# Attention and a maxout feed-forward: four visits to the scores in a group with four score banks, in place of three visits with six

## The chip, the cores and the metric

The kernel runs on one core of a Trainium2 chip. The core has TensorE for matmuls (PE in the profile; PEld is its loading of weights), VectorE (DVE), ScalarE (ACT), GpSimd (POOL) and SyncE (SP); here POOL and SP only issue transfers, apart from a few constants at the start. Matmuls write to PSUM, which has eight banks of 2 KB in each of 128 partitions; VectorE and ScalarE read them from there. The metric is the time of one execution on the device, in microseconds, the median over runs.

## What is computed

An attention whose softmax has one more term in the denominator, and then a feed-forward that takes the largest of three products:

```python
# q, k, v: (8 batches, 12 heads, 448 positions, 64)
scores = matmul(q, k.T) / sqrt(64)
m = max(scores);  e = exp(scores - m)
attn = e / (sum(e) + exp(-m) + 1e-9)
x = matmul(attn, v)                      # -> 3584 tokens x 768
h = maximum(maximum(x @ w1, x @ w2), x @ w3)      # 768 x 768 each
out = h @ w_out                          # 3584 x 768, float32
```

Without the maximum this is `exp(s) / (sum(exp(s)) + 1)`, and that is how the kernel computes it. It works in float16 with float32 sums.

## The kernel before

**Tiling.** The 12 heads of a batch are three groups of four; 8 batches make 24 groups, numbered `i` from 0 to 23. A batch has 448 positions, four chunks of 112 keys. Within a group, heads go in two pairs (`pr`), because two heads of 64 rows fill the 128 rows of TensorE.

**A group's steps.** `copy_qk` and `pair_qk` (L133 to L149) copy a pair's k and q on VectorE into the order that a transpose wants. The transpose runs on TensorE for groups below `PE_TR = 7` (`pe_transpose_pair`, L151, with a copy from PSUM to `qkT` at L162), later as a DMA on the SP queue (`dma_transpose_pair`, L165). `scores_visit` (L174) computes score units: a unit is a pair and a key chunk, two matmuls of 448 columns (L187) into a tile `stp` of two PSUM banks; then ScalarE takes the exponential of each tile into `eT` (L196). `av_group` (L205) makes three products of 16 matmuls each (L216), four at a time in 32 columns of TensorE: the denominator with a matrix of ones, and the even and the odd half of the numerator. VectorE copies each out of PSUM (`den` L226, `num` L231), ScalarE makes 1/(den + 1) as exp(-ln) (`lnd` L235, `rb` L237), and `normalize` (L239) multiplies into `xT`, two multiplications (L240).

**The feed-forward in pieces.** A batch's feed-forward is a list `pieces`: 18 up pieces (`up_piece`, six matmuls at L325 each, then a copy or a maximum into `hT` on VectorE, L333 and L335) and then output pieces (`out_piece`, six matmuls at L366, a scaling at L373, and stores on the SP queue at L389), six for an even batch and eight for an odd one. `moe(cols)` (L413) adds `cols` to a credit and issues pieces while the credit is above zero. After each piece it takes one job from the list `jobs`; jobs are VectorE's `normalize` steps and the copies and DMA transposes for the group after next, so that they do not stand in a row ahead of the pieces' evictions.

**PSUM.** `ps1` has two tiles of one bank (transposes, AV products, pieces), `ps2` two tiles of two banks and `ps3` one tile of two banks (both for `stp`; in batch 0 `ps3` holds the denominator). That is eight banks.

**Order.** The program is written in the order in which each engine is to run it; no scheduler moves it. Batch 0 is attended in two halves of the queries (`scores_half`, `av_half`), its order is a string of letters, `start` (L452), and its feed-forward is made of `up_half` pieces (L344). From group 3 on, a loop (L467) runs three visits in a group, with score units 0 to 2, 3 to 5, and 6 and 7:

```python
scores_visit(i, (0, 1, 2))
normalize = av_group(i - 1)          # from group 4 on; pieces in group 3
scores_visit(i, (3, 4, 5))
moe(gap)
next_pair(0)                         # moe(gap), with the transposes of the next groups
scores_visit(i, (6, 7))
moe(gap)
next_pair(1)
```

`add_pieces(b - 1)` runs in a batch's first group after `next_pair(0)`, and `gap` is then what the list holds, divided by 12 (a group has four calls of `moe(gap)`). After the loop follow the last AV, what is left in the list, and the last batch's feed-forward. The loads of q, k and v for group `i + 3` are issued at the head of group `i`, from POOL's queue.

Of the kernel before, what the change touches and what calls it, by code (L numbers as in the profile page):

```python
# [10 lines left out]
FP32 = mybir.dt.float32  # L11
FP16 = mybir.dt.float16
AF = mybir.ActivationFunctionType
ALU = mybir.AluOpType
ts = bass.ts

MMDT = FP16
# [4 lines left out]
def kernel(  # L22
# [11 lines left out]
    nc = tc.nc  # L34
# [30 lines left out]
    ht_pool = ctx.enter_context(tc.tile_pool(name="ht", bufs=2))  # L65
    out_pool = ctx.enter_context(tc.tile_pool(name="outp", bufs=3))

    ps1 = ctx.enter_context(tc.tile_pool(name="ps1", bufs=2, space=bass.MemoryType.PSUM))
    ps2 = ctx.enter_context(tc.tile_pool(name="ps2", bufs=2, space=bass.MemoryType.PSUM))
    ps3 = ctx.enter_context(tc.tile_pool(name="ps3", bufs=1, space=bass.MemoryType.PSUM))  # L70

    ctx.enter_context(tc.manual_schedule())

# [56 lines left out]

    state = {}

    def copy_qk(i, pr, n):  # L133
        st = state.setdefault(i, {"qk16": {}, "qkT": {}})
        if n == 0:
            st["qk16"][pr] = p16_pool.tile(
                [SC, 2, NCH, 2, D], MMDT, tag="qk16", name="qk16"
            )
        if i == 0 and pr == 0:
            src = first["kq"[n]]  # L140
        else:
            src = raw[i]["kq"[n]][:, 2 * pr : 2 * pr + 2]
        nc.vector.tensor_copy(
            out=st["qk16"][pr][:, n], in_=src.rearrange("p h c d -> p c h d")
        )

    def pair_qk(i, pr):
        for n in range(2):
            copy_qk(i, pr, n)  # L149

    def pe_transpose_pair(i, pr):  # L151
        st = state[i]
        qk16 = st["qk16"].pop(pr)
        trT = ps1.tile([128, 2, S], MMDT, tag="bank1", name="trT")
        for n in range(2):
            for c in range(NCH):
                nc.tensor.transpose(  # L157
                    out=trT[:, n, ts(c, SC)], in_=qk16[:, n, c, :, :],
                    identity=ident16[0:SC, 0:SC],
                )  # L160
        qkT = att_pool.tile([2 * D, 2 * S], MMDT, tag="qkT", name="qkT")
        nc.vector.tensor_copy(out=qkT, in_=trT.rearrange("p n s -> p (n s)"))  # L162
        st["qkT"][pr] = qkT

    def dma_transpose_pair(i, pr):  # L165
        st = state[i]
        qkT = att_pool.tile([2 * D, 2 * S], MMDT, tag="qkT", name="qkT")
        nc.sync.dma_start_transpose(
            out=qkT.rearrange("p (n s) -> p n s", s=SC),
            in_=st["qk16"].pop(pr).rearrange("p n c h d -> p (n c h d)"),  # L170
        )
        st["qkT"][pr] = qkT

    def scores_visit(i, units):  # L174
        st = state[i]
        if "eT" not in st:
            st["eT"] = e_pool.tile([SC, GH, NCH, S], MMDT, tag="eT", name="eT")
        stps = []
        for u in units:
            pr, c = divmod(u, NCH)  # L180
            qkT = st["qkT"][pr]
            if u in (2, 5):
                stp = ps3.tile([128, 2, 512], FP32, tag="bank3", name="stp")
            else:
                stp = ps2.tile([128, 2, 512], FP32, tag="bank2", name="stp")
            for hh in range(2):
                nc.tensor.matmul(  # L187
                    out=stp[:, hh, 0:S],
                    lhsT=qkT[hh * D : hh * D + D, c * SC : c * SC + 128],
                    rhs=qkT[hh * D : hh * D + D, S : 2 * S],  # L190
                    start=True,
                    stop=True,
                )
            stps.append((pr, c, stp))
        for pr, c, stp in stps:
            nc.scalar.activation(  # L196
                out=st["eT"][:, 2 * pr : 2 * pr + 2, c, :],
                in_=stp[0:SC, :, 0:S],
                func=AF.Exp,
                scale=scale,  # L200
            )
# [3 lines left out]
    def av_group(i):  # L205
        b, g = groups[i]
        st = state.pop(i)
        eT, v16 = st["eT"], raw[i].pop("v")
        if g == 0:
            xT[b] = xt_pool.tile([128, NDC, S], MMDT, tag="xT", name="xT")  # L210

        def col_tiled(weights):
            bank = ps1.tile([128, 512], FP32, tag="bank1", name="av")
            for c in range(NCH):
                for hh in range(GH):
                    nc.tensor.matmul(  # L216
                        out=bank[32 * hh : 32 * hh + 32, 0:S],
                        lhsT=weights(hh, c),
                        rhs=eT[:, hh, c, :],
                        start=(c == 0),  # L220
                        stop=(c == NCH - 1),
                    )
            return bank

        den = small.tile([128, S], FP32, tag="den", name="den")
        nc.vector.tensor_copy(  # L226
            out=den, in_=col_tiled(lambda hh, c: ones16[:, :])[:, 0:S]
        )
        num = small.tile([128, 2, S], FP32, tag="num", name="num")
        for hf in range(2):  # L230
            nc.vector.tensor_copy(  # L231
                out=num[:, hf], in_=col_tiled(lambda hh, c: v16[:, hh, c, hf::2])[:, 0:S]
            )
        lnd = small.tile([128, S], FP32, tag="lnd", name="lnd")
        nc.scalar.activation(out=lnd, in_=den, func=AF.Ln, bias=one_b)  # L235
        rb = small.tile([128, S], FP32, tag="rb", name="rb")
        nc.scalar.activation(out=rb, in_=lnd, func=AF.Exp, bias=ln_lam, scale=-1.0)  # L237

        def normalize(hf):  # L239
            nc.vector.tensor_tensor(  # L240
                out=xT[b][:, 2 * g + hf, :], in0=num[:, hf], in1=rb, op=ALU.mult
            )

        return normalize


    def scores_half(i, pr, half):
# [28 lines left out]
    def av_half(i, half):  # L276
# [6 lines left out]
        def col_tiled(out, weights):  # L283
# [7 lines left out]
                        stop=(c == NCH - 1),  # L291
                    )

        den = ps3.tile([128, 2, 512], FP32, tag="bank3", name="den")[:, 0]
        num = ps1.tile([128, 512], FP32, tag="bank1", name="num")
        col_tiled(den[:, 0:HQ], lambda hh, c: ones16[:, :])
        lnd = small.tile([128, S], FP32, tag="lnd", name="lnd")
        nc.scalar.activation(  # L298
# [3 lines left out]
        nc.scalar.activation(  # L302
            out=rb[:, 0:HQ], in_=lnd[:, 0:HQ], func=AF.Exp, bias=ln_lam, scale=-1.0
        )
        for hf in range(2):
            col_tiled(num[:, ts(hf, HQ)], lambda hh, c: v16[:, hh, c, hf::2])
        for hf in range(2):
# [91 lines left out]
    def add_pieces(b):  # L399
        for fc in range(NFC):  # L400
            for i in range(3):
                pieces.append((up_piece, (b, fc, i), NDC * (S + 6)))
        add_out(b)

    credit = [0.0]
    jobs = []

    def flush():
        while jobs:
            f, a = jobs.pop(0)  # L410
            f(*a)

    def moe(cols):  # L413
        credit[0] += cols
        while pieces and credit[0] > 0:
            f, a, w = pieces.pop(0)
            f(*a)
            credit[0] -= w
            if jobs:
                f, a = jobs.pop(0)  # L420
                f(*a)
        if not pieces:
            credit[0] = min(credit[0], 0.0)


    NI = len(groups)
    PE_TR = 7
    UP_H = 2 * NDC * (HQ + 6)
# [38 lines left out]
    for i in range(NG, NI):  # L467
        b, g = groups[i]
        if i == 3:
            load_group(5, "qk")  # L470
            load_group(4, "v")
            load_weight(3)
            load_group(5, "v")
            load_group(6)
        elif i + 3 < NI:
            load_group(i + 3)
        on_pe = i + 1 < PE_TR
        if i == NG:
            gap = sum(w for f, a, w in pieces) / 15

        def next_pair(pr):
            if i + 2 >= PE_TR and i + 2 < NI:
                for n in range(2):
                    jobs.append((copy_qk, (i + 2, pr, n)))
                jobs.append((dma_transpose_pair, (i + 2, pr)))
            if on_pe:
                pair_qk(i + 1, pr)
            moe(gap)
            if on_pe:
                pe_transpose_pair(i + 1, pr)  # L490

        scores_visit(i, (0, 1, 2))
        normalize = None
        if i > NG:
            normalize = av_group(i - 1)
        else:
            moe(gap)
        scores_visit(i, (3, 4, 5))
        if i > NG:
            for hf in range(2):  # L500
                jobs.append((normalize, (hf,)))
        moe(gap)
        next_pair(0)
        if i > NG and g == 0:
            flush()
            add_pieces(b - 1)
            gap = sum(w for f, a, w in pieces) / 12
        scores_visit(i, (6, 7))
        moe(gap)
        next_pair(1)  # L510
        flush()
    normalize = av_group(NI - 1)
    for hf in range(2):
        jobs.append((normalize, (hf,)))
    moe(float("inf"))
    flush()
    add_pieces(B - 1)
    moe(float("inf"))

# [29 lines left out]
```

## Time and profile before

| | before |
|---|---|
| median of 3 runs | 360.43 us (360.41 to 360.69) |
| the profiled execution's own time | 360.69 us |
| its span, first to last instruction | 358.9 us |
| granted TensorE clock | 0.999 |
| TensorE busy | 341.4 us, 3148 matmuls |
| VectorE busy | 213.4 us, 430 instructions |
| ScalarE busy | 192.7 us, 247 instructions |
| GpSimd busy | 58.1 us |
| DMA moved | 40.75 MB |

The profile is of one execution. Its page gives each engine's busy time, the span in 40 slices, and the chain of waits that ended last. In rows of instructions, a line such as "L325 PE MATMUL p_i<-xT" names the line of the kernel, the engine, the operation, the tile written and those read. A row of the timeline has the start, the duration, and in brackets how long the engine stood idle before it and what released it. In the chain in order of time, a row is the start, how long the chain lay there, and what ran: for TensorE one stretch of matmuls of the same line. Matmuls overlap each other in the array, so the duration of one (353 ns) is longer than the distance between two (189 ns).

### The profile page before, as it was taken

What the parts mean: (1) busy time and instruction counts of PE and PEld (TensorE: products, weight loads), DVE (VectorE), ACT (ScalarE), POOL (GpSimd) and SP (SyncE); (2) the same over time, 40 slices, a digit from 0 to 9 for tenths busy, and PEclk for the clock granted to TensorE, in tenths of its full rate; (3) what the DMA queues carried; (4) which work ended last, traced back from release to release, by engine and by line L of the source; (5) the groups of instructions that cost most, each with busy time, mean ns of one, the idle gap of its engine ahead of it and who ended that gap; (6) DMA issues with size and microseconds to landing.
All of it is one profiled execution on the core that took longest, in us unless ns stands there. A gap on an engine that the chain in (4) does not pass through costs nothing.

```text
span 358.9 us, 7470 instructions
## 1 busy us (share of the span) xinstructions
PE 341.4 (95%) x3148; PEld 178.2 (50%) x3148; DVE 213.4 (59%) x430; ACT 192.7 (54%) x247; POOL 58.1 (16%) x90
## 2 busy tenths in 40 slices
PE   3879899999999999999999999999999999999994
PEld 2557777544444444444444544444445444445552
DVE  3334566676666666665657657656656655656553
ACT  3697567875563664663762863763764664630000
POOL 8424532220220220220220220220000000000000
PEclk9999999999999999999999999999999999999999
DMA  9999999489746964857739876759421540012006
GB/s 137 193 208 206 202 199 161 59 171 162 102 66 124 179 125 75 118 107 161 103 57 122 150 166 101 102 99 188 53 54 26 136 118 2 0 46 88 2 4 173
DMA packets 71617, 40.75 MB, mean 114 GB/s; under 512 B 33824, under 2 KB 66848, under 8 KB 71584
## 3 DMA queue, kind: packets, MB, share of 16 engines
q0 software_dynamic: 35072, 21.01, 42.9%
q1 hardware_dynamic: 36272, 19.05, 22.2%
q8 instruction: 24, 0.39, 0.4%
q10 hardware_dynamic: 240, 0.23, 0.2%
q14 instruction: 9, 0.07, 0.1%
HBM read 42.47 MB, written 11.01 MB: 149 GB/s over the span
## 4 chain that ended last, share of the span: by engine, by line
PE 91%; ACT 2%; DVE 2%; DMA 2%; issue 1%; POOL 1%; DVEq 0%; POOLq 0%
PE p_i L325 41%; PE op_ps L366 15%; PE av L216 15%; PE stp L187 11%; PE p_i L344 6%; DMA ld_k<-in_k_dram 2%; PE trT L157 2%; ACT eTh L269 1%; PE stp L260 1%; PE num L286 1%; PE den L286 1%; ACT rb L302 0%; DVE xT L308 0%; ACT lnd L298 0%; DVE qkT L162 0%
## 5 line engine op out<-in xcount | busy, mean ns | idle before, releaser
L196 ACT ACTIVATE eT<-stp 112x896 f16<-112x896 f32 x168 | 141.9, 912 | 109.3 <-PE stp L187 109.3
L335 DVE TENSOR_TENSOR hT<-hT,p_i 128x448 f16<-128x448 f16 x84 | 52.2, 622 | 43.5 <-PE p_i L325 43.5
L366 PE MATMUL op_ps<-w_130,hT 128*128 128x384 f16 x336 | 57.9, 327 | 0.0
L325 PE MATMUL p_i<-xT,w_127 128*128 128x448 f16 x252 | 54.7, 353 | 0.0
L325 PE MATMUL p_i<-xT,w_129 128*128 128x448 f16 x252 | 54.6, 353 | 0.0
L325 PE MATMUL p_i<-xT,w_128 128*128 128x448 f16 x252 | 54.6, 353 | 0.0
L89 POOL DMA_DIRECT2D ld_v<-in_v_dram x24 | 17.0, 709 | 177.0 <-PE stp L187 171.8
L366 PEld LDWEIGHTS <-hT 128*128 128x128 f16 x336 | 31.6, 98 | 25.1 <-issue 3.0
L187 PE MATMUL stp<-qkT 64*128 64x448 f16 x336 | 42.7, 353 | 0.0
L373 DVE TENSOR_SCALAR o_sb<-op_ps 128x384 f32<-128x384 f32 x56 | 31.1, 556 | 18.4 <-PE op_ps L366 18.4
L216 PE MATMUL av<-eT,ld_v 112*32 112x448 f16 x672 | 38.8, 353 | 0.0
L333 DVE CAST hT<-p_i 128x448 f16<-128x448 f32 x42 | 26.2, 625 | 20.8 <-PE p_i L325 20.8
L325 PEld LDWEIGHTS <-w_127 128*128 128x128 f16 x252 | 23.6, 98 | 25.2 <-issue 4.4
L325 PEld LDWEIGHTS <-w_129 128*128 128x128 f16 x252 | 23.9, 98 | 24.7 <-issue 3.3
L325 PEld LDWEIGHTS <-w_128 128*128 128x128 f16 x252 | 23.9, 98 | 24.7 <-issue 3.3
L231 DVE COPY num<-av 128x448 f32<-128x448 f32 x42 | 26.2, 625 | 8.8 <-PE av L216 6.0
L269 ACT ACTIVATE eTh<-stp 112x896 f16<-112x896 f32 x24 | 20.5, 912 | 12.7 <-PE stp L260 12.6
L216 PEld LDWEIGHTS <-ld_v 112*32 112x32 f16 x672 | 18.6, 97 | 16.5 <-issue 5.0
L240 DVE TENSOR_TENSOR xT<-num,rb 128x448 f16<-128x448 f32 x42 | 25.9, 617 | 0.0
L187 PEld LDWEIGHTS <-qkT 64*128 64x128 f16 x336 | 11.3, 94 | 24.6 <-issue 19.1
L226 DVE COPY den<-av 128x448 f32<-128x448 f32 x21 | 13.1, 625 | 16.1 <-PE av L216 16.1
L216 PE MATMUL av<-eT,ones_121 112*32 112x448 f16 x336 | 19.8, 355 | 0.0
(161 smaller groups left out, 225.6 us busy)
## 6 DMA issues: line engine op xcount, KB each, us to landing
ld_v<-in_v_dram POOLq DMA_DIRECT2D x24, 224.0 KB, 4.1
ld_q<-in_q_dram POOLq DMA_DIRECT2D x23, 224.0 KB, 5.1
ld_k<-in_k_dram POOLq DMA_DIRECT2D x23, 224.0 KB, 6.1
out_dram<-o_sb SPq DMA_DIRECT2D x8, 336.0 KB, 3.0
out_dram<-o_sb SPq DMA_DIRECT2D x8, 288.0 KB, 3.8
out_dram<-o_sb SPq DMA_DIRECT2D x8, 240.0 KB, 3.4
out_dram<-o_sb SPq DMA_DIRECT2D x8, 192.0 KB, 2.7
w_127<-in_moe_w_dram POOLq DMA_DIRECT2D x3, 384.0 KB, 11.9
```

What stands on the lines that cost most here:

```text
L187: nc.tensor.matmul(out=stp[:, hh, 0:S], lhsT=qkT[hh * D : hh * D + D, c * SC : c * SC + 128], rhs=qkT[hh * D : hh * D + D, S : 2 * S], sta ...
L196: nc.scalar.activation(out=st["eT"][:, 2 * pr : 2 * pr + 2, c, :], in_=stp[0:SC, :, 0:S], func=AF.Exp, scale=scale,)
L216: nc.tensor.matmul(out=bank[32 * hh : 32 * hh + 32, 0:S], lhsT=weights(hh, c), rhs=eT[:, hh, c, :], start=(c == 0), stop=(c == NCH - 1),)
L231: nc.vector.tensor_copy(out=num[:, hf], in_=col_tiled(lambda hh, c: v16[:, hh, c, hf::2])[:, 0:S])
L240: nc.vector.tensor_tensor(out=xT[b][:, 2 * g + hf, :], in0=num[:, hf], in1=rb, op=ALU.mult)
L269: nc.scalar.activation(out=st[key][:, 2 * pr : 2 * pr + 2, 2 * n : 2 * n + 2, :], in_=stp[0:SC, :, 0:S].rearrange("p h (c q) -> p h c q", ...
L325: nc.tensor.matmul(out=p_i[:, 0:S], lhsT=w_sb[i][:, dc, ts(fc, 128)], rhs=xT[b][:, dc, :], start=(dc == 0), stop=(dc == NDC - 1),)
L333: nc.vector.tensor_copy(out=dst, in_=p_i[:, 0:S])
L335: nc.vector.tensor_tensor(out=dst, in0=dst, in1=p_i[:, 0:S], op=ALU.max)
L344: nc.tensor.matmul(out=p_i[:, ts(j, HQ)], lhsT=w_sb[i][:, dc, ts(2 * fp + j, 128)], rhs=xT[b][:, dc, ts(half, HQ)], start=(dc == 0), stop= ...
L366: nc.tensor.matmul(out=op_ps[:, 0:NW], lhsT=hT[bp][:, fc, ts(t, 128)], rhs=wout_sb[:, fc, ts(nh, NW)], start=(fc == 0), stop=(fc == NFC - 1),)
L373: nc.vector.tensor_scalar(out=o_sb[:, ts(nh, NW)], in0=op_ps[:, 0:NW], scalar1=1.0 / LAMBDA, scalar2=None, op0=ALU.mult,)
```

## The change

The loop from group 3 on gets four visits with two score units each: a pair and half of its key chunks (`visits`). The score tiles have four banks (`ps2` alone); `ps3` is gone, and `ps1` has four tiles. AV's three products are not copied out of PSUM: ScalarE reads the denominator there, and VectorE multiplies the numerators from there, at once and without the list of jobs, which is gone. The copies for a DMA transpose stand directly ahead of it. `add_pieces` comes right after the AV that ends a batch, ahead of the second visit. The amount of pieces in a visit follows from a fixed rate, `steady` (in group 3 from what is left of batch 0): the credit for the first visit is reduced by the columns of an AV, and where a transpose runs on TensorE its columns are taken off. `start` and the order of batch 0 stay as they are; its denominators go to `ps1` instead of `ps3`.

```diff
-    ps1 = ctx.enter_context(tc.tile_pool(name="ps1", bufs=2, space=bass.MemoryType.PSUM))
+    ps1 = ctx.enter_context(tc.tile_pool(name="ps1", bufs=4, space=bass.MemoryType.PSUM))
     ps2 = ctx.enter_context(tc.tile_pool(name="ps2", bufs=2, space=bass.MemoryType.PSUM))
-    ps3 = ctx.enter_context(tc.tile_pool(name="ps3", bufs=1, space=bass.MemoryType.PSUM))
...
     def dma_transpose_pair(i, pr):
+        pair_qk(i, pr)
...
-    def scores_visit(i, units):
+    def scores_visit(i, pr, cs):
...
-        for u in units:
-            pr, c = divmod(u, NCH)
-            qkT = st["qkT"][pr]
-            if u in (2, 5):
-                stp = ps3.tile([128, 2, 512], FP32, tag="bank3", name="stp")
-            else:
-                stp = ps2.tile([128, 2, 512], FP32, tag="bank2", name="stp")
+        for c in cs:
+            stp = ps2.tile([128, 2, 512], FP32, tag="bank2", name="stp")
...
-        den = small.tile([128, S], FP32, tag="den", name="den")
-        nc.vector.tensor_copy(
-            out=den, in_=col_tiled(lambda hh, c: ones16[:, :])[:, 0:S]
-        )
-        num = small.tile([128, 2, S], FP32, tag="num", name="num")
-        for hf in range(2):
-            nc.vector.tensor_copy(
-                out=num[:, hf], in_=col_tiled(lambda hh, c: v16[:, hh, c, hf::2])[:, 0:S]
-            )
+        den = col_tiled(lambda hh, c: ones16[:, :])
         lnd = small.tile([128, S], FP32, tag="lnd", name="lnd")
-        nc.scalar.activation(out=lnd, in_=den, func=AF.Ln, bias=one_b)
+        nc.scalar.activation(out=lnd, in_=den[:, 0:S], func=AF.Ln, bias=one_b)
...
-        def normalize(hf):
+        for hf in range(2):
+            num = col_tiled(lambda hh, c: v16[:, hh, c, hf::2])
             nc.vector.tensor_tensor(
-                out=xT[b][:, 2 * g + hf, :], in0=num[:, hf], in1=rb, op=ALU.mult
-            )
-
-        return normalize
+                out=xT[b][:, 2 * g + hf, :], in0=num[:, 0:S], in1=rb, op=ALU.mult
+            )
...
-        den = ps3.tile([128, 2, 512], FP32, tag="bank3", name="den")[:, 0]
-        num = ps1.tile([128, 512], FP32, tag="bank1", name="num")
+        den = ps1.tile([128, 512], FP32, tag="bank1", name="den")
...
+    UP = NDC * (S + 6)
+    OUT = NFC * (NW + 6)
+    steady = (3 * NFC * UP + 3.5 * NH * OUT) / NG
+    av_cols = 3 * NCH * (S + 6) + 480
+    tr_cols = 2 * NCH * SC
+    visits = [(pr, cs) for pr in range(2) for cs in ((0, 1), (2, 3))]
...
+        tr = tr_cols if i + 1 < PE_TR else 0
+        if g == 0:
+            per_group = sum(w for f, a, w in pieces) / NG if i == NG else steady
+        gap = (per_group + av_cols + 2 * tr) / 4
+        for vi, (pr, cs) in enumerate(visits):
+            if vi == 1 and i > NG:
+                av_group(i - 1)
+                if g == 0:
+                    add_pieces(b - 1)
+            scores_visit(i, pr, cs)
+            if vi == 0:
+                moe(gap - av_cols)
+            elif vi == 1:
+                moe(gap)
+            else:
+                if tr:
+                    pair_qk(i + 1, vi - 2)
+                moe((gap - tr) / 2)
+                if tr:
+                    pe_transpose_pair(i + 1, vi - 2)
+                if i + 2 >= PE_TR and i + 2 < NI:
+                    dma_transpose_pair(i + 2, vi - 2)
+                moe((gap - tr) / 2)
+    av_group(NI - 1)
+    add_pieces(B - 1)
+    moe(float("inf"))
```

More of the change, by code (lines that the diff above doesn't have):

```diff
@@ L131, with pair_qk @@
     state = {}
-    def copy_qk(i, pr, n):
+    def pair_qk(i, pr):
         st = state.setdefault(i, {"qk16": {}, "qkT": {}})
-        if n == 0:
-            st["qk16"][pr] = p16_pool.tile(
-                [SC, 2, NCH, 2, D], MMDT, tag="qk16", name="qk16"
-            )
-        if i == 0 and pr == 0:
-            src = first["kq"[n]]
-        else:
-            src = raw[i]["kq"[n]][:, 2 * pr : 2 * pr + 2]
-        nc.vector.tensor_copy(
-            out=st["qk16"][pr][:, n], in_=src.rearrange("p h c d -> p c h d")
-        )
-    def pair_qk(i, pr):
-        for n in range(2):
-            copy_qk(i, pr, n)
+        qk16 = p16_pool.tile([SC, 2, NCH, 2, D], MMDT, tag="qk16", name="qk16")
+        for n, name in enumerate("kq"):
+            if i == 0 and pr == 0:
+                src = first[name]
+            else:
+                src = raw[i][name][:, 2 * pr : 2 * pr + 2]
+            nc.vector.tensor_copy(
+                out=qk16[:, n], in_=src.rearrange("p h c d -> p c h d")
+            )
+        st["qk16"][pr] = qk16
     def pe_transpose_pair(i, pr):
+        if pr not in state.get(i, {"qk16": {}})["qk16"]:
+            pair_qk(i, pr)
         st = state[i]
@@ L165, in dma_transpose_pair @@
     def dma_transpose_pair(i, pr):
+        pair_qk(i, pr)
         st = state[i]
@@ L177, in scores_visit @@
             st["eT"] = e_pool.tile([SC, GH, NCH, S], MMDT, tag="eT", name="eT")
+        qkT = st["qkT"][pr]
         stps = []
-        for u in units:
-            pr, c = divmod(u, NCH)
-            qkT = st["qkT"][pr]
-            if u in (2, 5):
-                stp = ps3.tile([128, 2, 512], FP32, tag="bank3", name="stp")
-            else:
-                stp = ps2.tile([128, 2, 512], FP32, tag="bank2", name="stp")
+        for c in cs:
+            stp = ps2.tile([128, 2, 512], FP32, tag="bank2", name="stp")
             for hh in range(2):
@@ L193, in scores_visit @@
                 )
-            stps.append((pr, c, stp))
-        for pr, c, stp in stps:
+            stps.append(stp)
+        for c, stp in zip(cs, stps):
             nc.scalar.activation(
@@ L223, in col_tiled @@
             return bank
-        den = small.tile([128, S], FP32, tag="den", name="den")
-        nc.vector.tensor_copy(
-            out=den, in_=col_tiled(lambda hh, c: ones16[:, :])[:, 0:S]
-        )
-        num = small.tile([128, 2, S], FP32, tag="num", name="num")
-        for hf in range(2):
-            nc.vector.tensor_copy(
-                out=num[:, hf], in_=col_tiled(lambda hh, c: v16[:, hh, c, hf::2])[:, 0:S]
-            )
+        den = col_tiled(lambda hh, c: ones16[:, :])
         lnd = small.tile([128, S], FP32, tag="lnd", name="lnd")
-        nc.scalar.activation(out=lnd, in_=den, func=AF.Ln, bias=one_b)
+        nc.scalar.activation(out=lnd, in_=den[:, 0:S], func=AF.Ln, bias=one_b)
         rb = small.tile([128, S], FP32, tag="rb", name="rb")
         nc.scalar.activation(out=rb, in_=lnd, func=AF.Exp, bias=ln_lam, scale=-1.0)
-        def normalize(hf):
+        for hf in range(2):
+            num = col_tiled(lambda hh, c: v16[:, hh, c, hf::2])
             nc.vector.tensor_tensor(
-                out=xT[b][:, 2 * g + hf, :], in0=num[:, hf], in1=rb, op=ALU.mult
+                out=xT[b][:, 2 * g + hf, :], in0=num[:, 0:S], in1=rb, op=ALU.mult
             )
-        return normalize
     def scores_half(i, pr, half):
@@ L304, in av_half @@
         )
+        num = ps1.tile([128, 512], FP32, tag="bank1", name="num")
         for hf in range(2):
@@ L405 @@
     credit = [0.0]
[L406 to L411, printed above, removed]
     def moe(cols):
@@ L418, in moe @@
             credit[0] -= w
-            if jobs:
-                f, a = jobs.pop(0)
-                f(*a)
         if not pieces:
             credit[0] = min(credit[0], 0.0)
+    UP = NDC * (S + 6)
[4 more added lines that the diff above has]
+    visits = [(pr, cs) for pr in range(2) for cs in ((0, 1), (2, 3))]
     NI = len(groups)
@@ L476 @@
             load_group(i + 3)
[L477 to L516, printed above, removed]
+        tr = tr_cols if i + 1 < PE_TR else 0
[12 more added lines that the diff above has]
+                moe(gap)
+            else:
+                if tr:
[7 more added lines that the diff above has]
+    av_group(NI - 1)
     add_pieces(B - 1)
```

## The prediction

> **What bounds the kernel now.** I read the page first: engine shares, then the slices, then the chain that ended last, and from there the chain in order of time, where one step is one stretch of TensorE work.
>
> ```profile
> span 358.9 us, 7470 instructions
> PE 341.4 (95%) x3148; PEld 178.2 (50%) x3148; DVE 213.4 (59%) x430; ACT 192.7 (54%) x247; POOL 58.1 (16%) x90
> ...
> PE   3879899999999999999999999999999999999994
> ...
> PE 91%; ACT 2%; DVE 2%; DMA 2%; issue 1%; POOL 1%; DVEq 0%; POOLq 0%
> ```
>
> TensorE is the bound: 95% busy, 91% of the chain; every slice from the sixth to the last but one is full. The other engines are at 59% or less. So the change can only move three things: time in which TensorE waits, time that it loses between stretches, and the ends. In order of time (start, us, what), one steady group and the last feed-forward read:
>
> ```profile
> 100.31 0.67 PE stp L187 x6
> 100.99 2.54 PE av L216 x48
> 103.53 0.67 PE stp L187 x6
> 104.20 4.65 PE p_i L325 x24
> 108.85 0.48 PE stp L187 x4
> ...
> 325.62 20.43 PE p_i L325 x108
> ```
>
> The 108 matmuls at the end give 20.43/108 = 0.189 us each. Two score matmuls run side by side, so x4 is 2 steps, 0.378, and x6 is 3 steps, 0.568; the rows say 0.48 and 0.67. 24 pieces of up matmuls are 4.54; the row says 4.65. So **each stretch costs 0.10 to 0.11 us beyond its work**, whatever its length. AV (48 matmuls, 4 side by side) is 12 steps, 2.27; its row says 2.54, that is 0.27 over, 0.16 more than any other stretch. Where that comes from, the timeline of the same group shows:
>
> ```profile
> 101.91 0.62 DVE L226 COPY den<-av 128x448 f32<-128x448 f32 x1 [0.74 <-PE av L216]
> 102.59 0.50 PEld L216 LDWEIGHTS <-ld_v 112*32 112x32 f16 x15 [0.24 <-issue]
> ```
>
> The denominator's copy ends at 101.91 + 0.62 = 102.53; the weight loads of the third product, idle for 0.24, go on at 102.59. `ps1` has two banks, and the third product takes the denominator's. In the half-size AV of batch 0 only two banks are filled in all, and it shows no such excess (0.50 + 0.77 for 12 steps of 0.096: 0.12 over).
>
> More waits for banks or copies lie in the first 80 us. From the timeline:
>
> ```profile
> 36.07 0.69 DVE L308 TENSOR_TENSOR xT<-num,rb 128x224 f16<-128x224 f32 x2 [1.48 <-ACT rb L302]
> 36.81 0.56 PE L344 MATMUL p_i<-xT,w_128 128*128 128x224 f16 x4 [1.20 <-DVE xT L308]
> ```
>
> and, from the list of TensorE's waits (in all, times, longest):
>
> ```profile
> PE trT L157 <- DVE qk_1302 L143: 0.5, 1, 0.5
> PE trT L157 <- DVE qk_1117 L143: 0.3, 1, 0.3
> ```
>
> The first is again a bank: this piece reads parts of `xT` that were written 10 us earlier, but its bank is the one that `num` holds until the multiplication at 36.07 to 36.76. The last two are transposes that wait for their copies, which queue on VectorE behind a `normalize` job.
>
> **What the Trainium skill says.** "TensorEngine Tiling (Array Packing)", Key Properties: changing the tiling mode drains TensorE. Scores use 64 rows, AV 32 columns, the rest the whole array, so every stretch above begins with such a change; the trace agrees, at 0.10 to 0.11 us. "Perfetto Trace Analysis", Optimization Strategy: the same gap repeating on the saturated engine can mean that PSUM ran out for the next tile. That is AV's 0.16, 21 times. "PSUM — Partial Sum Buffer", Engine vs sequencer instructions: ScalarE and VectorE queues are strictly first in, first out; the trace agrees (each `lnd` starts when the scores' exponentials ahead of it end), and I use it for what queues behind `lnd` and `rb`.
>
> **The change part by part.** I wrote out both programs' TensorE order; the matmuls are the same 3148.
>
> *More stretches.* Before, a group from 4 on is S6 AV S6 M S4 M: six stretches (S scores, M pieces). After, it is S4 (M) AV S4 M S4 M S4 M: eight, and nine where the credit lets a piece run ahead of AV, which is so in 12 of the 20 groups 4 to 23. Group 3 and batch 0 keep their number. So 20 more S and 20 + 12 more M: 20 x 0.10 + 32 x 0.11 = **+5.5 us**, all on the path, as TensorE has nothing to hide it under.
>
> *Four banks in `ps1`.* The third product of AV no longer waits: 21 x 0.15 (0.27 less the 0.12 of the half-size one) = **-3.1**. The piece at 36.81 finds a free bank: from the last transpose (start 35.40, 0.05 later the next could start) to 36.81 that is **-1.35**; its weights and data are there, and what follows up to group 3 moves with it.
>
> *Copies.* The 42 + 21 copies of `num` and `den` go: 63 x 0.625 = 39 us of VectorE, worth nothing by themselves, as VectorE is at 59% and not waited for outside the places named. `num` and `den` stay in their banks instead until ScalarE and VectorE have read them. `normalize` and the copies for transposes lose the job queue. The transposes for groups 5 and 6 now have a piece or a stretch between copy and use; the waits at 59, 69.7 and 73.9 (starts 0.56, 0.81, 0.41 apart instead of 0.16 to 0.19) go: **-1.25**. One new one comes: in group 4's last visit no piece lies between the copies and the transpose. VectorE first evicts the piece before (0.53 to the next start), then copies (0.41 from the first copy to the transpose at 62.12 to 62.53): about 1.0 after the scores start, which last 0.48: **+0.5**. DMA transposes (SP queue): each is issued in the same visit region as before, more than a group ahead of use, landing in 2.6 to 5.9 us; the output stores that share SP's queue come at similar distances. POOL's loads keep their order. Both at nothing; the cover is about 20 us, and a transpose later than that would hold a score stretch.
>
> *Four score banks instead of six.* A visit may fill two tiles and must then find both evicted at the next visit. From the trace: exponentials start 0.41 after the first score matmul, 0.80 apart, so the first tile is free 1.4 and the second 2.2 after the visit's start. The shortest distance between visits in the new order is S4 and two output pieces, 0.48 + 2.06 = 2.54: enough, if ScalarE isn't late. `lnd` and `rb` (0.71 + 0.67) go ahead of the second visit's exponentials; without a piece ahead of AV, they end 3.4 after the first visit's start, and those scores are ready at 3.3: 0.1 late, absorbed. Only in group 3 do two visits follow at once (the credit ahead of AV is negative there and no AV runs): the second waits for both evictions, 2.2 + 0.28 against 0.87: **+1.6**. The pair of waits for `eTh` at 22 to 23 us (1.02 and 0.44) is the same pattern.
>
> *`xT` straight from PSUM.* At the first group of a batch the new feed-forward may start right behind AV and S4. Where nothing is left of the last one (groups 6, 12, 18), its first piece reaches the last parts of `xT` 3.65 and 3.84 after AV's start; `lnd`, `rb` and two multiplications (0.54 apart) give them at 3.6 and 4.2: 0.35 x 3 = **+1.0**. In groups 9, 15 and 21 an output piece comes first and covers it. At the end, 0.1. Bounds: nothing to 2.
>
> Sum: +5.5 - 3.1 - 1.35 - 1.25 + 0.5 + 1.6 + 1.0 = **+2.9 us**. The profiled execution took 360.69 (1.8 us around its span); it gives 363.6. The median is 0.26 lower: **363.3 us**.
>
> **Rivals.**
> *Forecast:* stretches cost what they cost now, bank waits go, slower by 2.9. Its own range, with group 3 at 1.0 to 1.8, `xT` at 0 to 2 and small waits: 361.6 to 365.3.
>
> *ScalarE becomes the bound at visits.* For it: four banks and `lnd`, `rb` in the queue; banks of `den` freed by ScalarE instead of VectorE. Against: the 0.34 margin of the shortest distance, and 54% load. If half of the 84 visits were 0.1 late, +4: 367; at 0.3, beyond 370.
>
> *Faster: the drain is not additive.* If more, shorter stretches cost less each, the bank waits decide. The gains are 5.7, the new waits 3.1; so below 2.6/52 = 0.05 us a stretch the kernel is faster; at 0.02 it takes 358.9. Against: the excess is equal for x4, x6 and x24.
>
> *Nothing:* gains and losses cancel within 0.7 us, about what a measurement of this kernel can tell from no change (0.2%). Its description names the two query halves and the hand-made order, and those lines stand in both kernels: what the diff changes is all above.
>
> **Numbers.** Forecast 0.73, ScalarE 0.12, faster 0.08, nothing 0.07. Slower by over 0.2% is forecast and ScalarE: 0.85; within 0.07; faster 0.08. The forecast's 361.6 to 365.3 leaves out a little over 2 in 10; up to 366.2 takes in the milder half of the ScalarE case.
>
> **What would show it.** After: AV stretches of 2.38 to 2.40 instead of 2.54; S4 rows of 0.48 four times in a group; PE waiting for `eT` once, about 1.6 at 42 to 45 us, and not again; the piece at 36.8 starting at 35.5; short waits for `xT` in three groups; VectorE near 174 us busy. Wrong if S4 rows grow over 0.5 in steady groups (ScalarE), or if M rows of 6, 12 and 18 show less than 0.1 over their work (the drain), or if TensorE waits for `qkT` (DMA).

## The result and the profile after

The changed kernel takes **363.13 us** (median of 4 runs, 362.50 to 363.52); the kernel before, run beside it, 360.56. The ratio is 1.0065, 95% interval 1.0042 to 1.0087: slower by 0.4 to 0.9%, that is by 1.5 to 3.1 us. The profiled execution took 362.50 with a span of 360.7; it is the fastest of the four.

From the page of the changed kernel: span, engine shares, TensorE by slices, and the chain by engine.

```profile
span 360.7 us, 7434 instructions
PE 343.3 (95%) x3148; PEld 173.5 (48%) x3148; DVE 177.5 (49%) x367; ACT 197.3 (55%) x247; POOL 58.1 (16%) x90
...
PE   3789899999999999999999999999999999999994
...
PE 89%; ACT 5%; DVE 3%; DMA 1%; issue 1%; DVEq 0%
```

TensorE is the bound as before, with the same 3148 matmuls. VectorE lost 36 us of busy time (213.4 to 177.5) and the kernel got slower; what the 39 us of copies are worth, e8 below shows.

The chain of the changed kernel in order of time (start, us, what), from one group's AV up to the next:

```profile
91.02 2.38 PE av L209 x48
93.40 0.48 PE stp L180 x4
93.89 2.38 PE p_i L308 x12
96.27 0.49 PE stp L180 x4
96.75 3.51 PE p_i L308 x18
100.26 0.48 PE stp L180 x4
100.75 2.38 PE p_i L308 x12
103.12 0.48 PE stp L180 x4
103.61 1.24 PE p_i L308 x6
```

Nine stretches where there were six (in eight of the 20 groups, where no piece runs ahead of AV, it is eight). AV is 2.38 instead of 2.54. Each of the four score rows is 0.48 or 0.49, so no visit waits for a tile here. The rows of pieces carry the same excess as the long ones did: 12 x 0.189 = 2.27 against 2.38, 18 x 0.189 = 3.41 against 3.51, 6 x 0.189 = 1.13 against 1.24.

The timeline around one AV shows why AV got shorter: its weight loads run through without a pause, and `lnd` reads the denominator straight from PSUM (start, us, engine, line).

```profile
104.78 0.50 PEld L209 LDWEIGHTS <-ones_118 112*32 112x32 f16 x16 [0.37 <-issue]
...
105.36 1.43 PEld L209 LDWEIGHTS <-ld_v 112*32 112x32 f16 x32
...
105.77 0.63 ACT L220 ACTIVATE lnd<-av,one_b 128x448 f32<-128x448 f32 x1 [0.59 <-PE av L209]
```

What TensorE waits for in the changed kernel (us in all, times, longest), the rows from group 3 on:

```profile
PE stp L180 <- ACT eT L189: 1.3, 2, 0.8
...
PE trT L153 <- DVE qk_1174 L140: 0.4, 1, 0.4
```

The wait for exponentials (`eT`) is there for one visit, group 3's second. The transpose is the one in group 4's last visit. No scores wait for a `qkT` that came by DMA. The waits for `xT` are too short to get a row; they show in the distances between matmuls, below.

**The sum, measured.** From the first score matmul of group 3 to the last matmul I took the distance of each matmul's start to the next in both traces and compared it with the plain one of its kind (0.189 us for 448 columns, 0.1625 for 384). A change of mode is a border at which TensorE divides its array in another way: 64 rows for scores, 32 columns for AV, the whole array for pieces and transposes. Work without any wait or change is 291.91 us in both kernels.

| term | predicted | measured | from |
|---|---|---|---|
| more stretches | +5.5 | +5.2 | 127 changes of mode, 0.110 each, become 179, 0.107 each |
| AV's third product | -3.1 | -3.08 | 21 gaps of 0.147, all gone |
| transposes behind their copies | -1.25 | -1.36 | 0.47, 0.65, 0.24, gone |
| group 4's last transpose | +0.5 | +0.50 | new |
| group 3's second visit | +1.6 | +1.60 | 0.98 and 0.62 |
| first pieces behind `xT` | +1.0 | +1.09 | three of 0.29, one of 0.23 at the end |
| output pieces behind `hT` | not seen | -0.20 | 7 gaps of 0.067 become 4 |
| sum from group 3 on | +4.25 | **+3.75** | 310.87 to 314.62 |
| piece at 36.8 us | -1.35 | -1.35 | follows its transpose at once |
| landing of the first loads | not seen | -0.6 | 0.4 at group 1's first transpose (9.98 instead of 10.38), 0.2 from there to 17 us |
| profiled execution | +2.9 | **+1.8** | 358.9 to 360.7 |

The 52 added changes would be 5.6 at 0.107; they measure 5.2 because the 127 became shorter too, mostly the borders from AV to scores (0.120 to 0.106). That it is the change of mode that costs, and not any change of work, the same distances show: at the 18 borders of the changed kernel where the work changes and the mode does not (up pieces, output pieces, transposes), the distance is the plain one to within 1 ns.

The piece that stood at 36.8 us, in the changed kernel:

```profile
34.47 0.57 PE L153 MATMUL trT<-ident_99,qk_638 112*128 112x112 f16 x8
34.87 1.31 PE L327 MATMUL p_i<-xT,w_125 128*128 128x224 f16 x12
```

The last row but one of the table is probably no effect of the change: the loads stand in the same order, and in the twelve profiles here, each of another kernel, that transpose starts between 9.98 and 11.17 us. It is not excluded, though: the six kernels with the change's order have it at 9.98 to 10.52, the six with the old order at 10.28 to 11.17. The medians, over several landings, differ by 2.57, which is near the +2.4 of the other rows; their interval, 1.5 to 3.1, holds both that and the +1.8.

### The profile page after: what moved, and what is told of

It is laid out like the page before. It is cut to its first block, busy times and chain, and to the rows that moved or that the text cites. A ratio compares the mean times of both kernels' runs of the same rounds, so it can differ in the third digit from the quotient of the medians.

```text
span 360.7 us, 7434 instructions
## 1 busy us (share of the span) xinstructions
PE 343.3 (95%) x3148; PEld 173.5 (48%) x3148; DVE 177.5 (49%) x367; ACT 197.3 (55%) x247; POOL 58.1 (16%) x90
## 4 chain that ended last, share of the span: by engine, by line
PE 89%; ACT 5%; DVE 3%; DMA 1%; issue 1%; DVEq 0%
PE p_i L308 40%; PE op_ps L349 16%; PE av L209 11%; PE stp L180 11%; PE p_i L327 6%; PE trT L153 2%; ACT eTh L252 2%; ACT eT L189 1%; PE stp L243 1%; DVE xT L225 1%; DMA first_k<-in_k_dram 1%; PE num L269 1%; ACT rb L222 1%; ACT lnd L220 1%; DVE qkT L158 1%
## 5 line engine op out<-in xcount | busy, mean ns | idle before, releaser
L189 ACT ACTIVATE eT<-stp 112x896 f16<-112x896 f32 x168 | 144.7, 914 | 106.6 <-PE stp L180 106.6
L349 PE MATMUL op_ps<-w_127,hT 128*128 128x384 f16 x336 | 59.0, 327 | 0.0
L180 PE MATMUL stp<-qkT 64*128 64x448 f16 x336 | 46.6, 355 | 1.3 <-ACT eT L189 1.3
L225 DVE TENSOR_TENSOR xT<-av,rb 128x448 f16<-128x448 f32 x42 | 24.3, 620 | 42.9 <-ACT rb L222 42.9
L308 PEld LDWEIGHTS <-w_125 128*128 128x128 f16 x252 | 23.4, 98 | 27.0 <-issue 7.0
L308 PEld LDWEIGHTS <-w_126 128*128 128x128 f16 x252 | 22.9, 98 | 27.0 <-issue 7.8
L308 PEld LDWEIGHTS <-w_124 128*128 128x128 f16 x252 | 23.3, 98 | 25.9 <-issue 5.9
L209 PE MATMUL av<-eT,ld_v 112*32 112x448 f16 x672 | 35.4, 353 | 0.0
L180 PEld LDWEIGHTS <-qkT 64*128 64x128 f16 x336 | 9.8, 94 | 30.0 <-issue 29.2
L220 ACT ACTIVATE lnd<-av,one_b 128x448 f32<-128x448 f32 x21 | 13.3, 635 | 9.4 <-PE av L209 9.4
L88 POOL DMA_DIRECT2D ld_q<-in_q_dram x24 | 17.0, 707 | 6.0 <-DMA w_125<-in_moe_w_dram 1.4
```

The costliest lines, as they stand in the source:

```text
L88: nc.gpsimd.dma_start(out=tiles[name][:, h0 : h0 + step].rearrange("p h c d -> p h (c d)"), in_=src[:, h0 : h0 + step],)
L180: nc.tensor.matmul(out=stp[:, hh, 0:S], lhsT=qkT[hh * D : hh * D + D, c * SC : c * SC + 128], rhs=qkT[hh * D : hh * D + D, S : 2 * S], sta ...
L189: nc.scalar.activation(out=st["eT"][:, 2 * pr : 2 * pr + 2, c, :], in_=stp[0:SC, :, 0:S], func=AF.Exp, scale=scale,)
L209: nc.tensor.matmul(out=bank[32 * hh : 32 * hh + 32, 0:S], lhsT=weights(hh, c), rhs=eT[:, hh, c, :], start=(c == 0), stop=(c == NCH - 1),)
L225: nc.vector.tensor_tensor(out=xT[b][:, 2 * g + hf, :], in0=num[:, 0:S], in1=rb, op=ALU.mult)
L308: nc.tensor.matmul(out=p_i[:, 0:S], lhsT=w_sb[i][:, dc, ts(fc, 128)], rhs=xT[b][:, dc, :], start=(dc == 0), stop=(dc == NDC - 1),)
```

## Experiments

Medians below come with the kernel before at 360.7 to 360.9 in the same runs.

**Banks without the fourth visit (e1_banks).** The kernel before with the change's banks alone.

```diff
-    ps1 = ... bufs=2
-    ps3 = ... bufs=1
+    ps1 = ... bufs=4
...
-            if u in (2, 5):
-                stp = ps3.tile(...)
-            else:
-                stp = ps2.tile(...)
+            stp = ps2.tile(...)
...                        # the exponential follows its unit's matmuls
-        den = ps3.tile(...)[:, 0]
+        den = ps1.tile(...)
```

> The kernel before with one thing of the change alone: four banks for scores and four for the rest, the three visits kept (a visit of three units then has two tiles, and each exponential stands right behind its unit's matmuls). My theory: the change needs its fourth visit because of the banks; a third unit must wait until the first tile is evicted, 0.41 + 0.92 + 0.06 = 1.4 us after the visit's start instead of 0.39, so 1.0 us in each of 42 visits of three units, +42; AV and the piece at 36.8 us gain 3.1 + 1.35 as in the change: about 398 us. Rival (the banks taken from the scores cost nothing, four are enough in any order): 360.5 - 4.4 = 356.

Measured: 400.08 us, ratio 1.108 (1.1016 to 1.1145). Its list of TensorE's waits begins:

```profile
PE stp L183 <- ACT eT L190: 36.8, 42, 0.9
```

42 waits: two visits of three units in each of 21 groups. In distances between matmul starts they are 0.98 in a group's first visit and 1.10 in its second, where `rb` runs ahead of the exponentials. Four banks are not enough for three units; the visits of two are what makes the banks affordable, and the stretches are their price.

**No piece ahead of AV (e3_ahead).** The changed kernel, twelve stretches fewer, the same work.

```diff
-                moe(gap - av_cols)
+                credit[0] += gap - av_cols
```

> The changed kernel with no piece ahead of AV: the credit of the first visit is kept and spent behind the second. That takes 12 stretches away (179 changes of mode to 167 from group 3 on) and moves no work off TensorE. My theory, a stretch costs 0.107 us: -1.3, so 361.8 where the changed kernel takes 363.1. Rival (short stretches hide their change of mode, or the time is lost to ScalarE at visits): no change, or slower, since AV follows the first visit at once in every group and the exponentials, lnd and rb of that visit crowd together: 363.1 to 365.

Measured: 361.93 us, ratio to before 1.0029 (1.0012 to 1.0047), against 1.0065 for the changed kernel. From group 3 on it is 313.58 instead of 314.62: 1.04 less, of which the twelve changes are 1.27 and three more gaps behind `hT` take 0.2 back. No new wait for ScalarE appears although every AV now follows its visit directly.

**Visits cut in two (e7_split).** The changed kernel, 56 stretches more.

```diff
-            scores_visit(i, pr, cs)
+            scores_visit(i, pr, cs[:1])
+            if vi > 1:
+                moe((gap - tr) / 4)
+                credit[0] -= (gap - tr) / 4
+            scores_visit(i, pr, cs[1:])
```

> The changed kernel with the third and fourth visit of a group cut in two, a unit each, and pieces between them: 56 more stretches (179 changes of mode to 235 from group 3 on), each with less work, and no more banks needed. My theory, 0.107 us a stretch: +6.0, so 369.1 where the changed kernel takes 363.1. Rival (ScalarE at the visits makes the loss, not the stretches): one unit a visit eases the score banks, so equal or faster, 362 to 363.1.

Measured: 371.86 us, ratio 1.0307 (1.0267 to 1.0347). Slower, as the theory of stretches has it and against the rival, but 2.7 more than its figure. TensorE's timeline shows where:

```profile
46.33 1.32 PE L327 MATMUL p_i<-xT,w 128*128 128x224 f16 x12
47.59 0.36 PE L180 MATMUL stp<-qkT 64*128 64x448 f16 x2
48.58 0.57 PE L153 MATMUL trT<-ident,qk 112*128 112x112 f16 x8 [0.62 <-DVE qk L140]
```

The piece that stood between copies and transpose now runs ahead of the copies, and four transposes (in groups 3 and 5) wait 0.64 to 0.70 each: 2.7 in all. What is left of the 8.60 from group 3 on is 5.9 for 56 changes, 0.106 each. So a change of mode costs the same next to a visit of one unit as next to one of two or three.

**AV's second product in a score tile (e4_avbank).** The kernel before; the third product then takes the other bank of `ps1`.

```diff
+            if two:
+                bank = ps2.tile([128, 2, 512], FP32, tag="bank2", name="av")[:, 0]
+            else:
                 bank = ps1.tile([128, 512], FP32, tag="bank1", name="av")
...
-                out=num[:, hf], in_=col_tiled(lambda ...)[:, 0:S]
+                out=num[:, hf], in_=col_tiled(lambda ..., hf == 0)[:, 0:S]
```

> The kernel before with AV's second product (the first of the numerator) in a score tile, so that the third finds the other bank of ps1 free; all else as it was. My theory: the third product no longer waits for the denominator's copy, 21 x 0.147 = -3.1: 357.4. Rival (the 0.15 us between the second and third product is no wait for a bank): 360.5. If the borrowed tile holds up the second visit's scores instead: 360 to 362, with a wait of PE stp for DVE num.

Measured: 357.77 us, ratio 0.9909 (0.9876 to 0.9942). All 21 gaps of 0.147 are gone and no other wait has come; from group 3 on it is 307.52 instead of 310.87, 3.08 of it in these gaps and 0.3 in the changes of mode (0.108 each instead of 0.110). The 0.16 in AV's row was a wait for a bank, and the change's other banks are not needed to remove it.

**A share of pieces for group 3's first visit (e2_group3).** The changed kernel; group 3 has no AV, so none is taken off its credit.

```diff
-        gap = (per_group + av_cols + 2 * tr) / 4
+        av = av_cols if i > NG else 0
+        gap = (per_group + av + 2 * tr) / 4
...
-                moe(gap - av_cols)
+                moe(gap - av)
```

> The changed kernel, where group 3, which has no AV, gives its first visit the same share of pieces as the others, so that a stretch of pieces stands between its first two visits (two more stretches, 179 to 181). My theory: the wait of 1.60 us of the second visit for the score tiles goes, 2 x 0.107 come: -1.4, 361.7 where the changed kernel takes 363.1. Rival (ScalarE is behind anyway at that place, after batch 0): the wait only moves to the next visit, 363.1.

Measured: 362.77 us, ratio 1.0051 (1.0028 to 1.0074): of the expected gain of 1.4 about 0.4 came. The wait for `eT` is gone from the list, and two others have come:

```profile
47.03 0.55 PE L180 MATMUL stp<-qkT 64*128 64x448 f16 x4
48.02 0.57 PE L153 MATMUL trT<-ident,qk 112*128 112x112 f16 x8 [0.43 <-DVE qk L140]
...
50.66 0.52 PE L153 MATMUL trT<-ident,qk 112*128 112x112 f16 x7 [0.43 <-DVE qk L140]
```

With other shares no piece falls between copies and transpose in group 3's third and fourth visit, and each transpose waits 0.50 beyond the change of mode, as group 4's does in the changed kernel. -1.60 + 2 x 0.107 + 2 x 0.50 = -0.39; from group 3 on it measures -0.40. My expectation left the transposes out.

**Copies out of PSUM put back (e8_copies).** The changed kernel with the old `den` and `num` copies, all else the same.

> The changed kernel with the copies of denominator and numerators out of PSUM put back (63 copies, 39 us more of VectorE); four banks in ps1 and everything else stay. My theory: the copies cost VectorE alone, and TensorE sees them only where it waits for xT: 0.1 longer at groups 6, 12 and 18, and 0.65 at the last AV, since ln then starts after the copy: +0.9, 364.0 where the changed kernel takes 363.1. Rival (VectorE's 39 us matter, as evictions of pieces come late): several us slower, 366 and more, with waits of pieces for DVE.

Measured: 364.27 us, ratio 1.0086 (1.0057 to 1.0115), 1.1 above the changed kernel. From group 3 on +1.15: the `xT` waits are 0.345 instead of 0.286 at groups 6, 12 and 18, and at the last AV 0.58 and 0.35 instead of 0.23; the rest is three gaps of 0.09 at the part of `xT` just before. In this order 39 us of VectorE's work are worth 1.1, and only where a piece waits for `xT`.

**Batch 0's numerators beside its denominators (e5_numbank), and the three edits together (e6_best).** The kernel before, to clear `ps1` for the piece at 36.8 us; e6 adds e4's edit and earlier copies for the transposes.

```diff
-        den = ps3.tile(...)[:, 0]
-        num = ps1.tile(...)
+        both = ps3.tile([128, 2, 512], FP32, tag="bank3", name="den")
+        den, num = both[:, 0], both[:, 1]
```

> The kernel before, where batch 0 has its numerators in the second bank of the denominator's tile instead of in ps1. My theory: the piece after the first transpose of group 3 (at 36.8 us) finds a free bank, -1.35: 359.3 where the kernel before takes 360.7. Rival (the piece waits for xT itself): no change. Second rival: the shared tile makes the next denominator wait for the last multiplication, slower.

> The kernel before with three edits: AV's second product in a score tile, batch 0's numerators beside its denominators, and the copies for transposes on TensorE ahead of the pieces that come before the transpose. Three visits and six score banks stay. My theory: the three bank and copy waits go and no stretch is added: -3.1 - 1.35 - 1.35 = -5.8: 354.9 where the kernel before takes 360.7. Rival (waits taken away come back behind: earlier copies hold up evictions, with only two banks for pieces): 356 to 358.

Measured: 368.84 us for e5 (ratio 1.0184, 1.0139 to 1.0228) and 363.82 for e6 (1.0064, 1.0042 to 1.0085). Both expectations failed, and on the same edit. The piece itself does what was expected: in e5 it starts at 43.68, 0.40 after its transpose at 43.28, so it was a bank and not `xT` that it waited for. But the numerators now wait, in e5's timeline of batch 0:

```profile
21.25 0.94 PE L286 MATMUL den<-eTh,ones 112*32 112x224 f16 x16
22.75 1.69 PE L286 MATMUL den<-eTh,ld_v 112*32 112x224 f16 x32 [0.55 <-ACT lnd L298]
```

and, from e5's list of TensorE's waits:

```profile
PE den L286 <- ACT lnd L298: 4.0, 6, 1.2
```

The program orders these accesses by tile and not by bank: the numerator's first matmul now waits until `lnd` has read the denominator in the other bank of the same tile. e5's second rival had the shared tile as a cause, but with another wait, which did not come. The list has 4.0 us in six waits, and group 3 starts 7.6 us later than before; the last section comes back to the rest. From group 3 on, e6 takes 306.14 instead of 310.87, -4.7, with no wait of any transpose left. So the other two edits held.

**The mended version (e9_best).** e6 with tiles of their own.

```diff
-        den = ps3.tile(...)[:, 0]
-        num = ps1.tile(...)
+        den = ps1.tile([128, 512], FP32, tag="bank1", name="den")
+        num = ps3.tile([128, 2, 512], FP32, tag="bank3", name="num")[:, 0]
...                                  # and e4's edit
         scores_visit(i, (3, 4, 5))
+        if on_pe:
+            pair_qk(i + 1, 0)
...
-            if on_pe:
-                pair_qk(i + 1, pr)
             moe(gap)
             if on_pe:
                 pe_transpose_pair(i + 1, pr)
+                if pr == 0:
+                    pair_qk(i + 1, 1)
```

> As e6_best, but batch 0 keeps denominators and numerators in tiles of their own: the denominator in ps1, where its bank is free as soon as ln has read it, the numerator in ps3. My theory: e6_best lost 7.6 us before group 3 alone, because its numerator matmuls waited for ln in the shared tile; with that gone, batch 0 gains 1.25 (the piece at 36.8 us waits for ln of the third half, 35.5, instead of for the multiplication) and the rest 4.7, as e6_best's own trace shows from group 3 on: 354.7 where the kernel before takes 360.7. Rival (the denominator in ps1 now holds up transposes or pieces in batch 0, which have two banks): 356 to 358.

Measured: **355.56 us**, ratio 0.9832 (0.9799 to 0.9865), faster than the kernel before by 1.4 to 2.0%, and 7.6 us below the changed kernel's median. Its timeline of batch 0 and its chain of a steady group:

```profile
36.05 0.57 PE L157 MATMUL trT<-ident,qk 112*128 112x112 f16 x8
36.57 1.31 PE L347 MATMUL p_i<-xT,w 128*128 128x224 f16 x12
```

```profile
98.86 2.38 PE av L219 x48
101.25 0.68 PE stp L187 x6
101.92 4.64 PE p_i L328 x24
106.57 0.48 PE stp L187 x4
```

The piece follows its transpose by 0.52 instead of 1.76, and AV is as short as in the changed kernel, with three visits and six stretches. It gets the change's gains without its fourth visit. It is 0.9 slower than expected: from group 3 on it takes the 306.14 that were expected, but in its profile group 3 starts only 0.1 earlier than before, mainly because group 1's first transpose came 0.8 later (11.17 instead of 10.38).

**The changed kernel mended (e10_mended).** Group 3's share, no piece ahead of AV, copies one stretch earlier.

> The changed kernel with three edits: the share of pieces in group 3's first visit (as in e2_group3), no piece ahead of AV from group 4 on (as in e3_ahead), and the copies for the transposes on TensorE a stretch of pieces earlier. My theory: 10 stretches less, -1.1; the second visit of group 3 does not wait, -1.6; no transpose waits for its copies, -0.5, and the two waits that e2_group3 brought do not come: 359.9 where the changed kernel takes 363.1. Rival (the waits move on to ScalarE once pieces no longer separate the first visit from AV): 361 to 362.

Measured: 360.15 us, ratio 0.9987 (0.9968 to 1.0006): level with the kernel before. From group 3 on 311.66, 2.96 less than the changed kernel. Its only waits of 0.1 or more there are the four for `xT`, 1.09.

## Why the prediction was right

It gave 363.3 us in a range of 361.6 to 366.2; the median is 363.13. That it came within 0.2 is partly luck: four runs spread over 1.0 us, and the measured terms without the landing of the loads sum to +2.4 where it had +2.9. But the way there held too, term by term (table above):

- **More stretches, +5.5.** Measured +5.2. 0.107 us a change held next to stretches of 6 to 24 matmuls of pieces and of one to three units (e3, e7), so the cost adds up, which the rival of a faster kernel denied. (The prediction's "24 pieces" of 4.54 us are 24 matmuls, four pieces; its sum is right.) The point from which that rival would win, 0.05 us, is less than half of it. The Trainium skill states in "TensorEngine Tiling (Array Packing)", Key Properties, that a change of tiling mode drains TensorE; the traces agree, and the size comes from them.
- **AV's third product, -3.1.** Measured -3.08, and e4 shows that it was the bank.
- **The piece at 36.8 us, -1.35.** In the changed kernel it starts 0.40 after the transpose's start, before 1.76. e5 (0.40) and e9 (0.52) show the same with other banks.
- **Four score banks.** The rival in which ScalarE holds up the visits did not come: one wait, at the place named and of the size named. e1 shows how near it is: with three units in a visit it is 44 us.
- **Copies of `den` and `num` at nothing.** e8 gives 1.1, all of it at `xT`: small against 39 us, but not nothing. The term of +1.0 for `xT` holds only without these copies. VectorE's busy time fell to 177.5 and not to about 174, as the rows that went had overlapped others by some 3 us.
- **Not seen.** Output pieces reach `hT` 0.2 later in all in the kernel before; and the loads at the start land up to 1.2 us apart from one profile to the next, so that a single profile could not show the 2.9 of the sum.

So the change traded 5.8 us of waits for 5.2 us of mode changes, and three kinds of new waits, 3.2 us, made the loss of 2.4, with the 0.2 at `hT`. e10 takes two of the three kinds and ten of the stretches away and is level.

## What to carry to other kernels

Where TensorE has no idle time, count the changes of tiling mode in its instruction order and multiply by their measured price: here fewer buffers for the scores forced more and shorter visits, and these, with the waits that they brought, cost more than the waits that the change removed. Look for an idle tile to borrow before changing the order: e4 removed the wait for a bank in that way and added no stretch. But give each product a tile of its own, as e5 and e9 show. When shares of interleaved work are changed, look again at each producer that used to have a piece between it and its consumer: a wait removed in one visit came back in the next two.

## What was not expected

In e5_numbank TensorE stands idle for 4.0 us in batch 0's six new waits (5.3 in distances between matmul starts), and yet group 3 began 7.6 us later (9 with the wait at 36.8 gone). Most of the rest is the rate of the matmuls. The same transposes and products in the kernel before:

```profile
19.04 0.57 PE L157 MATMUL trT<-ident_102,qk_327 112*128 112x112 f16 x8
19.54 0.57 PE L286 MATMUL den<-eTh,ones_121 112*32 112x224 f16 x16
```

take 0.57. In e5_numbank eight transposes take 0.93,

```profile
20.39 0.93 PE L157 MATMUL trT<-ident,qk 112*128 112x112 f16 x8
```

and so do the 16 denominator matmuls, 0.94 (the row at 21.25 above). Both kernels start at this slower rate. The kernel before leaves it at about 16.5 us, e5 at 32.8: there, in the middle of a stretch of pieces, the distance between matmuls of 224 columns falls from 0.187 to 0.096. Of the twelve kernels, the two with the shared tile leave the slower rate at 32.4 and 32.8, the other ten by 19.6. The Trainium skill, "TensorE: Matmul & The Clock Gate", What's actually happening, says that the array runs at half its clock until activity releases it. The halved distances fit that; that the pauses of 0.55 us in each group put the release off is a guess. The profile's row of the granted clock shows full speed in all these slices, so it does not show this, and no run here separates it from another cause.
